# Both batches together, products on two halves of the rows, values and state in blocks of 64 columns

## The chip, the cores and the metric

The kernel runs on one core of a Trainium2 chip. A core has a matrix engine (TensorE, PE in the rows), three engines for elementwise work (VectorE or DVE, ScalarE or ACT, GpSimd or POOL) and SyncE (SP), which here issues all transfers. Each engine works through its own instructions in order and waits on semaphores for others. TensorE multiplies a stationary operand (loaded first, PEld in the rows) with a moving one and adds into banks of its result memory. The metric is the device time of one execution in microseconds (us): 297.85 is the median of 3 runs (297.58 to 298.0).

## The reference

Three steps follow each other, for 2 batches of 768 tokens. The first is a gated memory over time with 8 heads of 40 features:

```
m_new = max(f[t] + m, i[t]);  f_stab = exp(f[t] + m - m_new);  i_stab = exp(i[t] - m_new)
C = f_stab * C + i_stab * outer(v[t], k[t]);   n = f_stab * n + i_stab * k[t]
y[t] = sigmoid(o[t]) * (C @ q[t]) / max(|n . q[t]|, 1)
```

The heads are put side by side as x (320 features). The second step is x + relu(norm(x) @ w_ch1) @ w_ch2, where norm takes mean and variance over the features and w_ch1 is 320 x 1280. The third is h = relu(x @ w_in) with w_in 320 x 1024, a convolution of h over three neighbouring tokens, h * sigmoid(conv), and a product with w_out (1024 x 320). All is float32.

## The kernel before

The 768 tokens are worked through in 6 chunks of 128 (index c) and, within each, in the 2 batches (index b). For a chunk the memory is not stepped token by token: scores of keys against queries (line 491, two heads at a time, one on rows 0 to 39 and one on rows 64 to 103) are multiplied on VectorE by a decay table `wt` (made by line 447 in the first two chunks, by lines 452 and 456 later) and then with the values (line 509, 41 columns a head: 40 and the sum n); the state carried in from earlier chunks adds line 507; line 544 makes the chunk's contribution to the state, and lines 551 and 555 update it. VectorE then normalises (519 to 536), TensorE transposes (570), and ScalarE and VectorE split the result into a high and a low part (574, 575), since the layers multiply in a float32 format with a short fraction: each product is high x high, low x high and high x low.

The first layer (`f1_unit`) works in units u of two blocks f of 128 hidden features, with both batches as 256 moving columns. `first_mm` contracts 320 rows as 128 + 128 + 64; the last 64 share one product with the low parts of the same weights, so a block takes 8 products (lines 583 to 587). ScalarE (607) and VectorE (609) take a unit's bank of 512 columns out, as high and low parts, and `second_mm` (592 to 594) multiplies them with w_ch2, 320 columns a product, 6 products a block, into two banks that collect over all units. Line 636 adds x, line 570 transposes again, and three chunks later (`LAG`) `f2_unit` does the same for the third step, with the convolution on ScalarE, VectorE and GpSimd between (683 to 718). The banks for first products are two, taken in turn (`slots`, "big").

The weights arrive in float64, as pairs of words: lines 343 to 346 turn them into float32, and 369 to 391 split them, during the first half of the time. Transfers are issued by SyncE in order, at line 253.

Every operation is recorded first (`Sched.op`) and then written out in the order of the table `ORDER`, which sets each engine's sequence; a "-" in it is a product with constants (line 802) that keeps TensorE busy at the start. Semaphores are set by the data, whatever the order.

Of the kernel before, what the change touches and what calls it, by code (L numbers as in the profile page):

```python
# [8 lines left out]
F32 = mybir.dt.float32  # L9
# [8 lines left out]
L = 128  # L18
# [6 lines left out]
WARM_START, WARM_END = 950.0, 45000.0  # L25
# [3 lines left out]

ORDER = """
10 6 2 35 11 12 4 14 5 88 44 34 20 95 43 21 160 22 23 102 24 25 - - - - - - - 52 33 26 27 13 19 29 3 28 30 7 159 36
89 116 38 17 37 9 15 45 90 18 281 16 31 39 91 47 8 0 40 46 92 54 55 48 109 53 49 41 93 58 57 32 56 97 276 94 96 69
42 59 294 60 50 51 61 62 63 123 70 98 64 161 65 99 104 71 72 73 66 74 75 100 76 80 103 77 78 67 1 79 - 85 162 68 164
165 82 86 105 173 167 83 87 106 117 84 - - - - 282 163 118 166 245 119 169 107 168 170 81 120 171 181 277 172 283
# [42 lines left out]


class Sched:

    LAT = {"A": dict(A=150, G=175, P=150, S=145, V=180), "V": dict(A=128, G=155, P=130, S=120, V=127),
           "G": dict(A=80, G=80, P=86, S=67, V=80), "P": dict(A=200, G=222, P=2, S=190, V=196),
           "S": dict(A=20, G=20, P=20, S=20, V=20)}

    def __init__(self):
# [783 lines left out]
```

## Time and profile before

| | |
|---|---|
| median of 3 runs | 297.85 us (297.58 to 298.0) |
| profiled execution: span from first to last instruction | 285.8 us |
| around the span (median less span; the page gives the profiled execution no other time of its own) | 12.05 us |
| TensorE busy | 276.1 us (97%), 2180 instructions |
| VectorE, ScalarE, GpSimd busy | 205.4, 176.6, 102.1 us |
| moved by transfers | 34.84 MB |

A product's record reaches from its start to the end of its results, and the next product starts long before that, so the records overlap: what a product costs TensorE is the distance from its start to the next start. In a row of the time line "x16" means that 16 like instructions were merged, and the time is that from the first start to the last end. A granted clock of 1.00 is TensorE's upper level of 2.4 GHz.

### The profile page before, as it was taken

What the parts mean: (1) busy time and instruction counts of PE and PEld (TensorE: products, weight loads), DVE (VectorE), ACT (ScalarE), POOL (GpSimd) and SP (SyncE); (2) the same over time, 40 slices, a digit from 0 to 9 for tenths busy, and PEclk for the clock granted to TensorE, in tenths of its full rate; (3) what the DMA queues carried; (4) which work ended last, traced back from release to release, by engine and by line L of the source; (5) the groups of instructions that cost most, each with busy time, mean ns of one, the idle gap of its engine ahead of it and who ended that gap; (6) DMA issues with size and microseconds to landing.
All of it is one profiled execution on the core that took longest, in us unless ns stands there. A gap on an engine that the chain in (4) does not pass through costs nothing.

```text
span 285.8 us, 5747 instructions
## 1 busy us (share of the span) xinstructions
PE 276.1 (97%) x2180; PEld 265.5 (93%) x2181; DVE 205.4 (72%) x442; ACT 176.6 (62%) x409; POOL 102.1 (36%) x147
## 2 busy tenths in 40 slices
PE   7989999899989999999999999999999999999995
PEld 3977999799989999999999999999999999999994
DVE  5899999974985497668966465785345669797581
ACT  3949877687659449932747635453336358677672
POOL 4514486556556632755020410020100102533540
PEclk9979999999999999999999999999999999999999
DMA  6993977964785487033540000100001000010011
GB/s 267 354 324 102 381 263 275 307 229 167 248 300 145 146 251 238 0 101 102 183 166 27 2 0 2 47 2 0 2 0 46 2 0 3 0 49 0 24 71 46
DMA packets 11860, 34.84 MB, mean 122 GB/s; under 512 B 1431, under 2 KB 5416, under 8 KB 11832
## 3 DMA queue, kind: packets, MB, share of 16 engines
q1 hardware_dynamic: 11832, 34.47, 35.2%
q8 instruction: 17, 0.28, 0.4%
q14 instruction: 11, 0.09, 0.1%
HBM read 32.46 MB, written 2.01 MB: 121 GB/s over the span
## 4 chain that ended last, share of the span: by engine, by line
PE 64%; DVE 23%; ACT 5%; DMA 4%; issue 2%; SPq 0%; POOL 0%; DVEq 0%; POOLq 0%; ACTq 0%
PE bk L592 8%; PE bk L593 8%; PE bk L594 8%; PE bk L583 7%; PE bk L585 6%; PE bk L584 6%; DVE c L555 4%; PE bk L491 4%; PE bk L509 3%; PE bk L586 3%; PE bk L587 3%; DVE xc L536 2%; DVE wt L498 2%; DMA wt<-gd 2%; PE bk L570 2%
## 5 line engine op out<-in xcount | busy, mean ns | idle before, releaser
L592 PE MATMUL bk<-w2h,uh 128*128 128x320 f32 x120 | 38.5, 321 | 0.0
L708 DVE SCALAR_TENSOR_TENSOR scr<-scr,cwr 128x256 f32<-128x256 f32 x70 | 33.5, 518 | 6.0 <-ACT scr L702 5.6
L594 PE MATMUL bk<-w2h,ul 128*128 128x320 f32 x120 | 37.1, 309 | 0.0
L593 PE MATMUL bk<-w2l,uh 128*128 128x320 f32 x120 | 37.0, 309 | 0.0
L583 PE MATMUL bk<-xth,w1h 128*128 128x256 f32 x120 | 35.6, 297 | 0.1
L585 PE MATMUL bk<-xtl,w1h 128*128 128x256 f32 x120 | 33.9, 282 | 0.0
L584 PE MATMUL bk<-xth,w1l 128*128 128x256 f32 x120 | 33.8, 282 | 0.0
L609 DVE SCALAR_TENSOR_TENSOR ul<-bk,uh 128x512 fp32r<-128x512 f32 x30 | 20.5, 687 | 14.4 <-ACT uh L607 14.3
L583 PE MATMUL bk<-rh,wih 128*128 128x256 f32 (+1 forms) x96 | 27.9, 290 | 0.3 <-DVE ul L609 0.3
L346 POOL TENSOR_TENSOR scr<-scr 128x640 int32<-128x640 int32 x14 | 18.4, 1316 | 24.9 <-DVE scr L345 9.7
L585 PE MATMUL bk<-rl,wih 128*128 128x256 f32 (+1 forms) x96 | 27.2, 283 | 0.0
L584 PE MATMUL bk<-rh,wil 128*128 128x256 f32 (+1 forms) x96 | 27.2, 283 | 0.0
L607 ACT ACTIVATE uh<-bk 128x512 fp32r<-128x512 f32 x30 | 17.6, 592 | 15.2 <-PE bk L587 10.3
L684 ACT ACTIVATE scr<-bk 128x512 f32<-128x512 f32 (+2 forms) x29 | 14.9, 518 | 17.3 <-PE bk L587 17.2
L456 ACT ACTIVATE wt<-wt,bcol 128x128 f32<-128x128 f32 x64 | 22.8, 394 | 3.8 <-POOL wt L452 3.7
L509 PE MATMUL bk<-vk,wt 128*128 128x41 f32 x192 | 24.6, 270 | 0.0
L509 PEld LDWEIGHTS bk<-vk,wt 128*128 128x128 f32 x192 | 24.0, 192 | 0.1
L583 PEld LDWEIGHTS bk<-xth,w1h 128*128 128x128 f32 x120 | 22.7, 189 | 0.9 <-DVE ul L609 0.2
L592 PE MATMUL bk<-woh,uh 128*128 128x320 f32 x74 | 23.1, 312 | 0.0
L592 PEld LDWEIGHTS bk<-w2h,uh 128*128 128x128 f32 x120 | 22.5, 188 | 0.5
L593 PE MATMUL bk<-wol,uh 128*128 128x320 f32 x74 | 22.9, 309 | 0.0
L594 PE MATMUL bk<-woh,ul 128*128 128x320 f32 x74 | 22.8, 308 | 0.0
(192 smaller groups left out, 839.6 us busy)
## 6 DMA issues: line engine op xcount, KB each, us to landing
vk<-in_vko_dram SPq DMA_DIRECT2D x12, 528.0 KB, 6.4
xy<-in_kq_dram SPq DMA_DIRECT2D x12, 512.0 KB, 5.0
wt<-gd SPq DMA_DIRECT2D x8, 512.0 KB, 3.7
scr<-in_w_dram SPq DMA_DIRECT2D x6, 640.0 KB, 7.0
stg<-in_w_dram SPq DMA_DIRECT2D x4, 640.0 KB, 12.0
scr<-in_win_dram SPq DMA_DIRECT2D x4, 640.0 KB, 4.2
scr<-in_wout_dram SPq DMA_DIRECT2D x4, 640.0 KB, 4.9
out_dram<-scr SPq DMA_DIRECT2D x12, 160.0 KB, 1.8
```

The lines of the kernel that those rows point to most:

```text
L346: op(G, 80 + 1.78 * n, [(rk, 0)], [(rk, 1)], lambda: gq.tensor_tensor(out=hi, in0=hi, in1=lo, op=ALU.add))
L456: lambda h=h: ac.activation(out=w[:, h, :], in_=w[:, h, :], func=AF.Exp, bias=bcol[:, c * 16 + r0 + h:c * 16 + r0 + h + 1]))
L509: pe.matmul(out=num[:, h * 41:(h + 1) * 41], lhsT=w[:, GROW[h], :], rhs=v1[:, h * 41:(h + 1) * 41], start=(c == 0), stop=(c == 0 or h == m ...
L583: pe.matmul(out=pv, lhsT=wh[:, k, fs], rhs=hi(k), start=(k == 0), stop=False)
L584: pe.matmul(out=pv, lhsT=wl[:, k, fs], rhs=hi(k), start=False, stop=False)
L585: pe.matmul(out=pv, lhsT=wh[:, k, fs], rhs=lo(k), start=False, stop=False)
L592: pe.matmul(out=a, lhsT=hi(b), rhs=wh[:, k, :], start=first, stop=False)
L593: pe.matmul(out=a, lhsT=hi(b), rhs=wl[:, k, :], start=False, stop=False)
L594: pe.matmul(out=a, lhsT=lo(b), rhs=wh[:, k, :], start=False, stop=last)
L607: op(A, da(512, True), [pk], [hk], lambda: ac.activation(out=uh[i], in_=pb, func=AF.Relu))
L609: lambda: ve.scalar_tensor_tensor(out=ul[i], in0=pb, scalar=0.0, in1=uh[i].bitcast(F32), op0=ALU.max, op1=ALU.subtract))
L708: ve.scalar_tensor_tensor(out=cvt()[:, j], in0=h[:, j, :, k:k + 128], scalar=cw_t[:, k, f0 + j:f0 + j + 1], in1=cvt()[:, j], op0=ALU.mult, ...
```

## The change

Each chunk's attention is written once for both batches: `wt`, `qt`, the state, x and their operations hold both, so that elementwise instructions have twice the columns and are half as many, and values, keys and queries come in one transfer for both batches (keys and queries one for each batch, on 40 rows). The 8 banks are 4 pairs (`pp`), one bank of a pair for each batch or block.

The products of the layers, the decay tables, the spread of the running maximum and the transposes are cut into halves of 64 rows, rows 0 to 63 and rows 64 to 127. In `first_mm` and `second_mm` neighbouring instructions belong to different halves and to different banks of a pair; in phase 0 bank 0 takes the lower rows and bank 1 the upper, in phase 1 it is exchanged. 320 rows are 5 blocks of 64: three in one phase, two in the other. `mul` watches each bank: when a product comes from the other half of the rows than the one before it in that bank, an empty instruction of SyncE (`sp.nop`) waits for the last products of both banks, and the new product waits for it. From the second chunk on `f1_unit` takes two units at a time (`QUAD`) into one pair of banks, which it uses alone (`pair("big", [0])`). Values and state (`fnum`, `fst`) keep all 128 rows, and are cut into blocks of 64 result rows (`CB`), that is 64 columns of the stationary operand. The weights of the input layers lie by 64 rows, and one instruction splits them where there were three. The last output is taken out by ScalarE for one batch and by VectorE for the other. `ORDER` is new, with 1008 operations for 1252, and 26 of its entries are products with constants, each now two halves.

```diff
+QUAD = True
+CB = 64
...
+3 5 2 6 19 11 20 21 22 7 13 154 81 23 8 10 24 12 25 155 26 67 28 4 33 27 18 82 68 34 29 138 - - - - - - - - - - 37 36
...
+    pp = [ps.tile([128, 2, 512], F32, name=f"pp{i}", tag=f"pp{i}") for i in range(4)]
...
+    def pair(cls, slots):
+        n = count.get(cls, 0)
+        count[cls] = n + 1
+        i = slots[n % len(slots)]
+        return ("pp", i), pp[i]
...
+    def rows(h):
+        return slice(64 * h, 64 * h + 64)
...
+    def mul(**kw):
+        o, rg = kw["out"], kw["lhsT"].start_partition()
+        k = o.tensor.name, o.offset % 1024 // 512
+        if k in last and last[k][0] != rg and last[k][2] is None:
+            mark = sp.nop()
+            for q in range(2):
+                if (k[0], q) in last:
+                    r, old, _ = last[k[0], q]
+                    after(mark, old)
+                    last[k[0], q] = r, old, mark
+        mark = last[k][2] if k in last and last[k][0] != rg else None
+        ins = pe.matmul(**kw)
+        if mark:
+            after(ins, mark)
+        last[k] = rg, ins, None
...
+        def fnum():
+            for b in range(2):
+                for n in range(3 if c else 0):
+                    for z in range(0, 128, CB):
+                        pe.matmul(out=num[z:z + CB, b, n * 123:(n + 1) * 123], lhsT=qt[:, b, n, z:z + CB], rhs=ct[:, b, n * 123:(n + 1) * 123],
+                                  start=(n == 0), stop=False)
+                for n in range(NH):
+                    for z in range(0, 128, CB):
+                        pe.matmul(out=num[z:z + CB, b, n * 41:(n + 1) * 41], lhsT=w[:, b, GROW[n], z:z + CB], rhs=v1[:, b, n * 41:(n + 1) * 41],
+                                  start=(n == 0 and c == 0), stop=(n == NH - 1))
+        op(P, [(wk, 0), (wk, 1), (vkey, "v")] + (["ct", "qt"] if c else []), [nk], fnum)
...
+            def fst():
+                for b in range(2):
                     for g in range(3):
-                        pe.matmul(out=gb[0:120, g * L:(g + 1) * L], rhs=g80[0:32], start=True, stop=True,
-                                  lhsT=hsel[:, 360 * b + 120 * g:360 * b + 120 * g + 120])
-                op(P, 3 * 224 + 390, ["g80", "hsel"], [gk], feg, act=0.5)
-                op(A, da(384, True), [gk], [(ek, j) for j in range(3)],
...
+    def first_mm(t, pvs, wh, wl, n, hi, lo, ph, first, final):
+        if first:
+            fresh(t)
+        count = [0, 0]
+        for j in range(3 - ph):
+            for x, y in ((wh, hi), (wl, hi), (wh, lo)):
+                for bk in range(2):
+                    r, k = rows(bk ^ ph), ((0, 1, 2), (0, 2, 1))[bk ^ ph][j]
+                    a = x[r, n, j * 256 + bk * 128:j * 256 + bk * 128 + 128] if j < 2 else x[r, n, 512:640]
+                    count[bk] += 1
...
+    def second_mm(acc, hi, lo, wh, wl, fs, ph, first, final):
+        if first:
+            fresh(acc)
+        for n, f in enumerate(fs):
+            for x, y, m in ((hi, wh, 0), (hi, wl, 1), (lo, wh, 2)):
+                for b in range(2):
+                    r = rows(b ^ ph)
+                    mul(out=acc[:, b, 0:DM], lhsT=x(f, b, r), rhs=y[r, f, :],
+                        start=(first and n == 0 and m == 0), stop=(final and n == len(fs) - 1 and m == 2))
+
+    turn = {}
+
+    def phases(which, us):
+        p = turn.get(which, 0)
+        turn[which] = 1 - p
+        return [(u, p) for u in us] + [(u, 1 - p) for u in reversed(us)]
+
+    def f1_unit(c, us):
...
+        pk, pt = pair("big", [0])
+        nq = len(us)
...
+        todo = phases("f", list(range(nq)))
+        for n, (q, ph) in enumerate(todo):
+            u = us[q]
+            op(P, [("xth", c % 2), ("xtl", c % 2), ("w1", "h", u), ("w1", "l", u)], [pk],
+               lambda q=q, u=u, ph=ph, n=n: first_mm(pt, [pt[:, bk, q * 256:(q + 1) * 256] for bk in range(2)], w1h, w1l, u,
...
+    def f2_out(c):
+        a = pp[acc2(c)]
+        dst = out[:, c * L:(c + 1) * L, :].rearrange("b t d -> t b d")
+        if c < NC - 1:
+            op(A, [("pp", acc2(c))], ["ob"], lambda: ac.activation(out=ob, in_=a[:, :, 0:DM], func=AF.Copy, scale=0.5))
+            op(SP, ["ob"], [("out", c)], lambda: sp.dma_start(out=dst, in_=ob))
+        else:
+            op(A, [("pp", acc2(c))], [("ob", 0), "ob"], lambda: ac.activation(out=ob[:, 0], in_=a[:, 0, 0:DM], func=AF.Copy, scale=0.5))
+            op(V, [("pp", acc2(c))], [("ob", 1), "ob"] if 0 else [("ob", 1)],
+               lambda: ve.tensor_scalar(out=ob[:, 1], in0=a[:, 1, 0:DM], scalar1=0.5, scalar2=None, op0=ALU.mult))
             for b in range(2):
-                for j in range(nf):
```

In TensorE's order a second layer's products and a first layer's, in the fourth chunk of the first layer. Before (`bk_136` and `bk_137` collect the second products of the two batches, `bk_132` is one of two banks for first products):

```order
L592 MATMUL bk_136<-w2h,uh_125 128x320 [waits Activation_49]
L593 MATMUL bk_136<-w2l,uh_125 128x320
L594 MATMUL bk_136<-w2h,ul_129 128x320 [waits DVE_49]
L592 MATMUL bk_137<-w2h,uh_125 128x320
L593 MATMUL bk_137<-w2l,uh_125 128x320
L594 MATMUL bk_137<-w2h,ul_129 128x320
L583 MATMUL bk_132<-xth_117,w1h 128x256
L584 MATMUL bk_132<-xth_117,w1l 128x256
L585 MATMUL bk_132<-xtl_119,w1h 128x256
```

After, near the same place (`pp_111` is the pair for first products, `pp_113` and `pp_114` collect second products; line 233 is `mul`):

```order
L233 MATMUL pp_111<-xth_104,w1h 128x256 x2
L233 MATMUL pp_111<-xth_104,w1l 128x256 x2
L233 MATMUL pp_111<-xtl_106,w1h 128x256 x2
L233 MATMUL pp_114<-woh,uh 128x320 [waits SP_sequencer_49]
L233 MATMUL pp_114<-woh,uh 128x320
L233 MATMUL pp_114<-wol,uh 128x320 x2
L233 MATMUL pp_114<-woh,ul 128x320 x2
L233 MATMUL pp_114<-woh,uh 128x320 x2
L233 MATMUL pp_114<-wol,uh 128x320 x2
L233 MATMUL pp_114<-woh,ul 128x320 x2
L233 MATMUL pp_111<-xth_104,w1h 128x256 [waits SP_sequencer_49]
L233 MATMUL pp_111<-xth_104,w1h 128x256
```

Products now stand in twos, one of each half of the rows; a phase of second products (12 instructions) stands between the two phases of a first layer's unit, and both it and the second phase wait for SyncE.

The values of one chunk, before, for the first of the two batches (`c_96` is its state, `qt_88` its queries) up to where the other batch's begin:

```order
L507 MATMUL bk_135<-c_96,qt_88 128x123 [waits DVE_49,Pool_49]
L509 MATMUL bk_135<-vk_87,wt_92 128x41 [waits DMAHW4_49]
L509 MATMUL bk_135<-vk_87,wt_92 128x41 x2
L507 MATMUL bk_135<-c_96,qt_88 128x123
L509 MATMUL bk_135<-vk_87,wt_92 128x41 x3
L507 MATMUL bk_135<-c_96,qt_88 128x123
L509 MATMUL bk_135<-vk_87,wt_92 128x41 x2
L507 MATMUL bk_134<-c_97,qt_89 128x123 [waits DVE_49]
```

After, for both batches (line 472 is the state's part, line 476 the scores'):

```order
L472 MATMUL pp_112<-ct,qt 64x123 [waits DVE_49,Pool_49]
L472 MATMUL pp_112<-ct,qt 64x123 x5
L476 MATMUL pp_112<-vk_85,wt 64x41 [waits DMAHW1_49]
L476 MATMUL pp_112<-vk_85,wt 64x41 x15
L472 MATMUL pp_112<-ct,qt 64x123 x6
L476 MATMUL pp_112<-vk_85,wt 64x41 x16
```

Each product of 128 result rows has become two of 64, and the two batches follow each other in one group.

SyncE's issues in the first part of the program, before:

```order
L253 DMA scr<-in_w_dram 128x1280 [waits DMAHW7_49,DVE_49,Pool_49]
L336 DMA gd<-g_80 80x128 [waits DMAHW0_49,DVE_49]
L253 DMA scr<-in_w_dram 128x1280 [waits DMAHW1_49,DVE_49,Activation_49]
L253 DMA vk_85<-in_vko_dram 128x1056 [waits DMAHW2_49,PE_49]
L253 DMA xy_82<-in_kq_dram 128x1024 [waits DMAHW3_49]
```

After:

```order
L243 DMA scr<-in_w_dram 128x1280 [waits PE_49,DMAHW2_49,DVE_49,Activation_49]
L243 DMA stg_71<-in_w_dram 128x1280 [waits DMAHW3_49,DVE_49]
L314 DMA gd<-g_80 64x128 [waits PE_49,DMAHW4_49]
L243 DMA stg_72<-in_w_dram 128x1280 [waits DMAHW5_49,DVE_49,Activation_49]
L243 DMA vk_84<-in_vko_dram 128x2112 [waits DMAHW6_49,PE_49]
L243 DMA kq<-in_kq_dram 40x2048 [waits PE_49,DMAHW7_49]
```

There are 66 issues and the like instead of 88 rows, and a wait for PE in front of an issue is often that of an exchange signal, which the rows don't show by itself, standing in the queue between two issues.

## Rows read from the trace of the kernel before

**Rows 1.** The page: busy us and share of TensorE, and the chain's shares by engine.

```profile
PE 276.1 (97%) x2180; PEld 265.5 (93%) x2181; DVE 205.4 (72%) x442; ACT 176.6 (62%) x409; POOL 102.1 (36%) x147
PE 64%; DVE 23%; ACT 5%; DMA 4%; issue 2%; SPq 0%; POOL 0%; DVEq 0%; POOLq 0%; ACTq 0%
```

**Rows 2.** Stages: length; busy PE, PEld, DVE, ACT, POOL; granted clock; DMA share; GB/s.

```profile
0.00:23.40 23.40, 20.63 (x144) 15.81 (x145) 18.62 (x57) 14.39 (x29) 9.77 (x19) 0.93 0.89 311
23.40:60.00 36.60, 35.05 (x285) 32.26 (x285) 33.93 (x60) 29.98 (x67) 22.09 (x20) 1.00 0.76 270
60.00:160.00 100.00, 98.01 (x806) 95.87 (x805) 73.28 (x169) 63.67 (x165) 44.14 (x60) 1.00 0.47 155
160.00:282.50 122.50, 122.46 (x952) 121.60 (x951) 79.60 (x161) 68.12 (x150) 26.14 (x49) 1.00 0.04 15
```

**Rows 3.** Time line of TensorE at 161 us: start, us, engine, line, operation.

```profile
160.96 0.28 PE L587 MATMUL bk<-xtl,w1h 128*128 128x256 f32 x1
161.08 0.31 PE L592 MATMUL bk<-woh,uh 128*128 128x320 f32 x1
161.22 0.31 PE L593 MATMUL bk<-wol,uh 128*128 128x320 f32 x1
...
161.81 0.31 PE L594 MATMUL bk<-woh,ul 128*128 128x320 f32 x1
162.05 1.16 PE L491 MATMUL bk<-xy 40*128 40x128 f32 x16
163.14 0.39 PE L583 MATMUL bk<-rh,wih 128*128 128x256 f32 x1
163.36 0.28 PE L584 MATMUL bk<-rh,wil 128*128 128x256 f32 x1
```

**Rows 4.** The page's groups: busy us, mean ns, idle before and its releaser.

```profile
L592 PE MATMUL bk<-w2h,uh 128*128 128x320 f32 x120 | 38.5, 321 | 0.0
L583 PE MATMUL bk<-xth,w1h 128*128 128x256 f32 x120 | 35.6, 297 | 0.1
L609 DVE SCALAR_TENSOR_TENSOR ul<-bk,uh 128x512 fp32r<-128x512 f32 x30 | 20.5, 687 | 14.4 <-ACT uh L607 14.3
L607 ACT ACTIVATE uh<-bk 128x512 fp32r<-128x512 f32 x30 | 17.6, 592 | 15.2 <-PE bk L587 10.3
```

**Rows 5.** Time line of TensorE: values and state, at 12 and at 177 us.

```profile
12.61 0.88 PE L544 MATMUL bk<-vk 128*120 128x123 f32 x6
13.32 1.88 PE L509 MATMUL bk<-vk,wt 128*128 128x41 f32 x16
...
177.21 0.38 PE L507 MATMUL bk<-c,qt 120*128 120x123 f32 x2
177.42 0.76 PE L509 MATMUL bk<-vk,wt 128*128 128x41 f32 x6
...
179.58 0.37 PE L583 MATMUL bk<-xth,w1h 128*128 128x256 f32 x1
```

**Rows 6.** Time line at 148 us, where TensorE waits for VectorE.

```profile
148.57 0.69 DVE L609 SCALAR_TENSOR_TENSOR ul<-bk,uh 128x512 fp32r<-128x512 f32 x1 [1.60 <-ACT uh L607]
149.31 0.19 PEld L583 LDWEIGHTS bk<-rh,wih 128*128 128x128 f32 x1 [0.55 <-DVE ul L609]
149.31 0.39 PE L583 MATMUL bk<-rh,wih 128*128 128x260 f32 x1 [0.34 <-DVE ul L609]
```

**Rows 7.** Time line of the end.

```profile
282.11 0.83 ACT L740 ACTIVATE scr<-bk 128x320 f32<-128x320 f32 x2 [2.60 <-PE bk L594]
282.15 0.31 PE L594 MATMUL bk<-woh,ux 128*128 128x320 f32 x1
282.57 0.81 SPq L742 DMA_DIRECT2D out_dram<-scr  x2
```

**Rows 8.** The first layer's start in the time line.

```profile
23.36 0.39 PE L583 MATMUL bk<-xth,w1h 128*128 128x256 f32 x1
```

**Rows 9.** The page's transfers: count, KB each, us from issue to landing.

```profile
vk<-in_vko_dram SPq DMA_DIRECT2D x12, 528.0 KB, 6.4
...
stg<-in_w_dram SPq DMA_DIRECT2D x4, 640.0 KB, 12.0
```

More of the change, by code (lines that the diff above doesn't have):

```diff
@@ L109, in op @@
         deps.discard(i)
-        self.ops.append((eng, dur, deps, fn, dma))
-        if port is None:
-            port = not dma and dur > 0 and (eng == "G" or eng == "V" and not any(
-                isinstance(k, tuple) and k[0] == "bank" for k in list(reads) + list(writes)))
-        self.port.append(port)
-        if eng == "P":
-            self.act[i] = act
-    def chain(self, eng, steps, reads, writes, port=None):
-        for dur, fn in steps:
-            self.op(eng, dur, reads, writes, fn, port=port)
+        self.ops.append((eng, deps, fn))
     def emit(self, warm):
@@ new lines, in sm, with after @@
+    def sm(c):
+        return pair("sm", [1, 3]) if c <= 3 else pair("sm1", [1])
+    def rows(h):
+        return slice(64 * h, 64 * h + 64)
+    last = {}
+    def after(ins, old):
+        tc.add_manual_dep(ins.ins, old.ins.name, mybir.DependencyInfo(mybir.DependencyClass.Sync, mybir.DependencyReason.DATA))
+    def mul(**kw):
[13 more added lines that the diff above has]
+        last[k] = rg, ins, None
@@ L259, in consts, with fresh, load @@
+    def fresh(t):
+        for q in range(2):
+            last.pop((t.tensor.name if hasattr(t, "tensor") else t.name, q), None)
+    def load(dst, src, key, reads=(), e=None):
+        op(SP, list(reads), [key] if not isinstance(key, list) else key, lambda: (e or sp).dma_start(out=dst, in_=src))
+    op(V, [], ["one"], lambda: ve.memset(one, 0.0))
+    op(A, [], ["one"], lambda: ac.activation(out=one, in_=one, func=AF.Exp))
+    load(early[1][0:16, 0:2 * S], gf, "fi")
     def consts():
         make_identity(nc, ident)
-    op(G, 510, [], ["ident"], consts)
@@ L340, in convert, with spread @@
-    def convert(raw, n, rk):
+        load(f80, gf80, "f80")
+        mk, mb = sm(0)
+        m80 = mb[0:80, 0, 0:256].rearrange("p (k t) -> p k t", k=2)
+        def spread():
+            fresh(mb)
+            for k in range(2):
+                for n, c in enumerate(LATER):
+                    mul(out=m80[:, k, :], lhsT=zsel[:, 64 - 16 * n:144 - 16 * n], rhs=mm[:, c * L + k:(c + 1) * L + k],
+                              start=(n == 0), stop=(n == NC - 2))
+        op(P, ["m0", "m1", "mm0", "zsel"], [mk], spread)
@@ new lines, in gates_rest, with feg @@
+        gk, gb = sm(0)
+        def feg():
+            fresh(gb)
+            for g in range(3):
+                for b in range(2):
+                    mul(out=gb[0:120, b, g * L:(g + 1) * L], rhs=g80[64:128], start=True, stop=True,
+                              lhsT=hsel[:, 360 * b + 120 * g:360 * b + 120 * g + 120])
+        op(P, ["g80", "hsel"], [gk], feg)
+        op(A, [gk], EG,
+           lambda: ac.activation(out=eg, in_=gb[0:120, :, 0:384].rearrange("p b (g t) -> p b g t", g=3), func=AF.Exp))
@@ L606, in f1_unit @@
[L606 to L616 removed]
+        un[0] += nq
@@ L667, in f2_unit @@
         if c % 2:
-            rd = [r for r in rd if r[1] == 1] + [("r", 0, "x", 0), ("r", 0, "x", 1)]
-        pk, pb = pbank("big" if c < NC - 3 else "end")
-        late = c >= NC - 3
+            rd = [r for r in rd if r[1] == 1] + [("r", 0, "x")]
+        late = c >= NC - LAG
+        pk, pt = pair("end", [0, 1]) if late else pair("big", [0])
         i = un[0] % (9 if late else 4)
@@ L752, in dst_x @@
-    def dst_x(c, b):
-        sl = slice(b * 128, (b + 1) * 128)
-        return (lambda: xth[c % 2][:, :, sl], lambda: xtl[c % 2][:, :, sl], ("xth", c % 2, b), ("xtl", c % 2, b))
-    xinfo = {}
-    def attn(c):
-        todo = [attention(c, b, dst_x(c, b)) for b in range(2)]
-        while todo:
-            todo = [t for t in todo if next(t, 0) is None]
-    attn(0)
+    load(gln_t, gln.partition_broadcast(128), "gln")
+    attention(0)
     weights1()
     gates_rest()
-    load(cwr.rearrange("p n k -> p (n k)"), cw.bitcast(I32), [("cwr", 0), ("cwr", 1)], 128 * 192)
@@ L767, in tile_kernel, with zero_tail @@
-    convert(cwr, 24, "cwr")
-    op(G, 0, [("cwr", 1)], ["cw"], lambda: None)
+    load(cwr.rearrange("p n k -> p (n k)"), cw.bitcast(I32), [("cwr", 0), ("cwr", 1)])
+    convert(cwr, "cwr")
+    op(G, [("cwr", 1)], ["cw"], lambda: None)
     weights2()
+    def zero_tail():
+        gq.memset(rh()[:, :, :, 257:258].bitcast(F32), 0.0)
+        gq.memset(rl()[:, :, :, 257:258].bitcast(F32), 0.0)
     for s in range(NC + LAG):
-        a = [("a", u) for u in range(5)] if s < NC else []
-        f = f2_units(s - LAG) if s >= LAG else []
+        a = ([(n,) for n in range(5)] if s == 0 or not QUAD else [(0, 1), (2, 3), (4,)]) if s < NC else []
+        f = range(4) if s >= LAG else []
@@ L800, in tile_kernel @@
     with tc.manual_schedule():
         def warm():
-            pe.matmul(out=bank[7], lhsT=wz[:, 0:128], rhs=wz, start=True, stop=True)
-        sch.emit((WARM_START, WARM_END, warm))
+            for i in range(2):
+                mul(out=pp[2][:, i], lhsT=wz[rows(i), 0:128], rhs=wz[rows(i)], start=True, stop=True)
+        sch.emit(warm)
 _OUTS = [((2, 768, 320), 'float32')]
```

777 lines of the change are left out of this document (339 added, 438 removed), and 73 rows, old and new, of the table ORDER.

## The prediction, made before the result was known

> **What bounds the kernel now.** I read the page's busy shares first, then the chain that ended last, then a table of stages, then the time line of TensorE in the dense part. TensorE is busy for 276.1 of 285.8 us, and it holds 64% of the chain; VectorE, the next, holds 23% [rows 1]. A busy TensorE is not yet a TensorE at its limit, so the stages decide. Up to 23.40 us it waits for the head (transfers, the gate scan, the first chunk) and for its clock (granted 0.93); from 23.40 to 60.00 us VectorE works 33.93 of 36.60 us beside it; from 60.00 us on TensorE works 98.01 of 100.00 and then 122.46 of 122.50 us, at a granted clock of 1.00 (2.4 GHz), and VectorE has a third of its time free [rows 2]. So from 60 us on the sum of TensorE's steps is the time, and before that nearly so. The step from one start to the next is what counts, not the record's length, since records overlap: a first product (256 columns) takes 0.12 us, a second product (320 columns) 0.146 us (5 steps from 161.08 to 161.81) [rows 3]. The difference, 0.027 us for 64 columns, is 0.42 ns a column, so a first product is 0.107 us of columns and 0.013 us of something between two products.
>
> The page gives the profiled execution's span, 285.8 us; the median of the runs is 297.85, so 12.05 us lie around the span. I add the terms to the span and keep those 12.05 us.
>
> **The change, part by part.** All steps are between starts, in us.
>
> *First products.* Before, 8 in each of 108 blocks (60 of the first layer, as x120 with two a block shows, and 48 of the second) [rows 4]: 864 x 0.120 = 103.7. The 64 left-over rows share one product with their own low parts. After, the 5 blocks of 64 rows give 15 products for each bank, two at a time on the two halves of the rows: 54 units x 15 = 810 pairs. What a pair costs no row shows in this type. The nearest rows: the score products already run in pairs on rows 0 to 39 and 64 to 103, and 16 of them take 1.16 with their last record of 0.27, 0.89 for 8 pairs, 0.111 a pair [rows 3]; a whole product of the type in question costs 0.120. They are equally near (one has the tiling, the other the type), so I take the middle, 0.1155: 93.6, **-10.1**, with ends -13.8 and -6.5.
>
> *Second products.* 108 blocks x 6 = 648 steps before and 648 pairs after, so only the 0.013 between products is at stake: with the score pairs' 0.004 a step is 0.137, else 0.147; middle 0.142, **-3.3**, ends -6.5 and 0.
>
> *Values and state in halves of 64 columns.* Before, the values of one batch and chunk take 2.37 (177.21 to 179.58), 10 times, and 16 x 0.11 without the state term, 2 times; the state takes 0.88 less its last record, 0.7, 10 times [rows 5]: 34.2. A 41-column step costs 0.11 although its columns last 0.034 (twice 41 at 0.42 ns; two passes in this type), so the load of 128 columns sets it. A half loads 64 columns, 0.058. If the halves run beside each other as the score pairs do, a batch and chunk has 16 x 0.058 + 6 x 0.109 = 1.58, the first chunk 0.93, the state 0.65: 15.8 + 1.9 + 6.5 = 24.2, **-10.0**. If their loads go one after the other: 22 x 0.111 = 2.44, and 34.7 in all, +0.5. If nothing overlaps: 3.17, 3.7 and 13.1, +14.3. I take the first, by the score pairs' row, the only one in which TensorE is divided.
>
> *Changes of the tiling.* From the last whole product at 161.81 to the second at 163.36 one visit to the score pairs lasts 1.55; its steps are 0.147 + 8 x 0.111 + 0.120 = 1.155 [rows 3]. So two changes cost 0.40. In the order such changes fall from 30 to 18 (scores, transposes and layers now share one tiling): **-2.4**.
>
> *The exchange waits (new).* Each bank takes its first half of a sum from one half of the rows and the rest from the other. Between them TensorE signals SyncE, which signals back: 93 times. I counted in the order what TensorE does between, at the steps above: nothing in 13 cases, at least 0.66 us in 80. The price with nothing between: the last record 0.31, a hop 0.05 each way (VectorE's result ends at 149.26, the load starts at 149.31), SyncE's own step (no row shows one; between nothing and the 0.40 of an issue [rows 7], near nothing, 0.03, as it moves no data), the bare load 0.11 (the first record after a wait is 0.39, not 0.28), less the step of 0.147 [rows 3, 6]: 0.40. So 13 x 0.40 = **+5.2**; the 0.66 covers the price of the others. Ends +2.6 (half of it lies in waits that are there anyway) and +15 (0.12 for each covered one as well, the bare load alone).
>
> *One pair of banks for the first products (new).* Before, two banks take turns; after, a unit of 1024 columns fills both, and the next must wait for ScalarE and VectorE. By twice the 512-column rows that is 1.18 + 1.37 [rows 4], with record, hops and bare load under 3.0. The order puts 0.8 to 5.0 us of second products and attention between; over the 36 hand-overs some 3 us stay open: **+3.0**, ends 0 and +8. Both engines have room from 60 us on [rows 2].
>
> *The end and the head.* Before, the first batch's output leaves while the second is computed, ScalarE ends 0.5 us after the last product and two issues take 0.81 [rows 7]. After, both batches end together and the issues follow: **+0.4**. The first layer starts at 23.36 us [rows 8] behind the transfer of values and the chain on VectorE; after, the merged transfer (twice 528 KB [rows 9]) stands behind an exchange wait on SyncE, while the key transfers shrink. I take **0**, with 2 either way.
>
> *VectorE and ScalarE* do the same columns in fewer instructions. It costs nothing while TensorE covers them, and shortens the 23 to 60 us stage, where VectorE would else be next.
>
> Sum: -10.1 - 3.3 - 10.0 - 2.4 + 5.2 + 3.0 + 0.4 = -17.2. Span 268.6, time **280.6 us**.
>
> **The rivals.**
> 1. *Pairs without the gap.* If the pairs of the layers step like the score pairs, the two product terms are -20.3 instead of -13.4: 273.7 us. For it: the tiling is the same. Against: the gap of 0.013 belongs to the layers' type.
> 2. *The halves of 64 columns don't run beside each other.* Their outputs share a bank and their inputs the same rows, which no row before shows. With loads in turn the term is +0.5: 291.1 us; with nothing overlapping 304.9. Against: the loads of whole value products already hide behind products on the same rows, since a step of 0.11 is the load alone, not 0.107 + 0.034 [rows 5].
>  The Trainium skill ("TensorE: Matmul & The Clock Gate", Part 3, on what overlaps) says that a load overlaps running products only where the row group differs; by it the halves, which share all rows, would wait for each other and this rival would hold. The trace of before disagrees for whole products, and no row shows it for halves.
> 3. *Slower: the exchange waits stand in SyncE's queue behind transfers.* That queue goes in order, and 30 of the 93 signals follow an issue that itself waits for a buffer or an earlier transfer. If TensorE reaches the second half first, it stands for the rest of that wait; a landing takes 6.4 us for the values and 12.0 us for staged weights [rows 9]. It decides from 17.2 us: three or four such stops of 4 to 5 us. With 20 us the time is 300.6. For it: transfers are busy for half of the first 160 us (0.89, 0.76, 0.47) [rows 2]. Against: most issues wait for things that are long done when TensorE gets there, and from 160 us on the share is 0.04.
> 4. *The change doesn't do what it says:* two halves in the layers' type never run at once. Then 1458 pairs become 2916 steps, about +180 (1458 more at some 0.12): 460 us. The score pairs speak against it.
>
> **How the numbers follow.** Forecast 0.45 (own range 274 to 288, from the ends of the product and exchange terms); rival 1 0.26; rival 2 0.14; rival 3 0.13; rival 4 0.02. The forecast and rival 1 are faster; of rival 2 0.08 is still faster by over 0.2%, about what a measurement of this kernel can tell from no change, and 0.02 within it; I leave 0.01 of the forecast within it too. Faster 0.78, same 0.03, slower 0.19. For 8 in 10 the range goes from 267 (rival 1 with cheaper exchanges) to 299 (most of rival 2, the beginning of rival 3).
>
> **What would show it right or wrong.** In the profile after: pair steps of the layers between 0.111 and 0.120 and between 0.137 and 0.147; value steps of 41 columns at 0.06 a pair of halves, not 0.11; gaps of about 0.4 us on TensorE in front of 13 second halves and none in front of most others; a TensorE whose idle time is spread in small pieces. The forecast fails if a value pair takes 0.11 or more, if SyncE holds TensorE for microseconds, or if the dense part is set by VectorE or ScalarE.

## The result, and the profile after

The kernel after takes 287.68 us (median of 4, 286.36 to 289.03), the kernel before 297.93 in the same comparison (297.58 to 298.45): a ratio of 0.9657, 95% interval 0.9614 to 0.9699. Forecast were 280.6 and a range of 267 to 299. The sign and the range held, but much of the working behind them did not. One thing must be known to read the number: executions of the kernel before fall in two groups, 286 to 292 us and 295 to 301 (28 and 55 of the 83 that the experiments timed); all four in the comparison are of the long group, and the profile shown before the prediction is of the short one.

The kernel after, its page: busy time of the engines with share of the span, and the chain that ended last by engine, to be read against [rows 1].
```profile
span 287.3 us, 9346 instructions
...
PE 268.4 (93%) x4057; PEld 252.1 (88%) x4057; DVE 197.8 (69%) x343; ACT 164.3 (57%) x316; POOL 102.6 (36%) x133
...
PE 60%; DMA 13%; ACT 11%; DVE 8%; issue 4%; POOL 3%; SPq 1%; POOLq 0%; ACTq 0%; DVEq 0%
```
TensorE is 7.7 us less busy than before and yet the span is 1.5 us longer than the 285.8 of [rows 1]. Transfers hold 13% of the chain that ended last, where they held 4%. The stages say where the time went. The kernel after, by stretch; PEclk is the granted clock as a share of 2.4 GHz, the figures behind it the transfers' share and GB/s.
```profile
0.00:23.20 23.20, 15.88 (x170) 10.96 (x172) 13.04 (x29) 11.67 (x17) 9.31 (x19) 0.89 0.86 282
23.20:36.80 13.60, 12.98 (x126) 11.52 (x124) 8.67 (x25) 6.76 (x12) 3.74 (x3) 0.68 0.64 170
36.80:60.00 23.20, 23.00 (x379) 21.51 (x377) 17.15 (x26) 16.50 (x25) 14.35 (x11) 1.00 0.80 270
60.00:160.00 100.00, 96.26 (x1600) 92.92 (x1598) 76.25 (x118) 58.96 (x124) 50.26 (x56) 1.00 0.45 148
160.00:283.00 123.00, 120.31 (x1800) 115.23 (x1798) 82.21 (x147) 69.97 (x139) 24.90 (x45) 1.00 0.06 20
```
The first layer starts at 36.78 us, not at 23.36 [rows 8]. Up to 23.2 TensorE works 15.9 us, and from there to 36.8 at a clock of 0.68. This is the way there; TensorE, ScalarE (ACT), GpSimd (POOL) and SyncE's issues in the head of the kernel after, in order of engine.
```profile
14.95 0.85 PE L507 MATMUL pp<-vk 128*64 128x123 f32 x12 [0.36 <-POOL vk L449]
20.16 1.49 PE L507 MATMUL pp<-vk 128*64 128x123 f32 x12 [4.36 <-POOL half L261]
21.44 3.59 PE L476 MATMUL pp<-vk,early 128*64 128x41 f32 x64
...
36.78 0.28 PE L233 MATMUL pp<-xth,w1h 64*128 64x256 f32 x2
...
16.86 0.76 ACT L335 ACTIVATE stg<-stg 128x640 f32<-128x640 f32 x1 [4.70 <-DMA stg<-in_w_dram]
...
18.20 0.75 ACT L452 ACTIVATE vk<-vk 128x640 f32<-128x640 f32 x1
...
13.86 1.03 POOL L449 TENSOR_TENSOR vk<-vk,d 128x360 f32<-128x360 f32 x1 [2.07 <-DMA vk<-in_vko_dram]
...
19.02 1.09 POOL L449 TENSOR_TENSOR vk<-vk,d 128x360 f32<-128x360 f32 x1 [3.98 <-ACT vk L452]
...
7.54 0.36 SPq L243 DMA_DIRECT2D vk<-in_vko_dram  x1
```
Read from the bottom: the values of chunk 0 are issued at 7.54, behind two weight blocks and an exchange mark (before: 2.58), and GpSimd, which waits for them, starts at 13.86. ScalarE waits 4.70 us for a weight block; the tanh on the output gate, queued behind it, starts at 18.20. GpSimd's second scaling of the keys waits for that tanh, although it touches other columns. By the code, both batches now share one tile, and the gate's stretch over both encloses the second batch's keys; e3 moves that tanh. TensorE stands from 15.8 to 20.16 for it. Behind this wait the clock stands at its lower level (0.51 on average from 18 to 32), and the 64 value products take 3.59 us; in e3_gate_early, below, at the higher level they take 2.01.

The dense part of the kernel after: first products, second products, carried state (123 columns) and values (41).
```profile
48.48 0.86 PE L472 MATMUL pp<-ct,qt 120*64 120x123 f32 x12
49.17 1.08 PE L476 MATMUL pp<-vk,wt 128*64 128x41 f32 x32
50.07 0.83 PE L472 MATMUL pp<-ct,qt 120*64 120x123 f32 x12
...
53.20 0.28 PE L233 MATMUL pp<-xth,w1l 64*128 64x256 f32 x2
53.32 0.29 PE L233 MATMUL pp<-xtl,w1h 64*128 64x256 f32 x2
53.45 0.30 PE L233 MATMUL pp<-w2h,uh 64*128 64x320 f32 x2
53.59 0.31 PE L233 MATMUL pp<-w2l,uh 64*128 64x320 f32 x2
53.74 0.31 PE L233 MATMUL pp<-w2h,ul 64*128 64x320 f32 x2
```
A pair of first products steps by 0.12, a pair of second ones by 0.146, hardly less than the whole products of [rows 3]. A batch's 16 value products, as 32 halves, go by in 0.90 (49.17 to 50.07): 0.056 a pair of halves, against 0.11 [rows 5]. The forecast of the halves was right, and the Trainium skill ("TensorE: Matmul & The Clock Gate", Part 3, on what overlaps), by which a load overlaps running products only where the row group differs, does not hold here: all these halves use the same rows, and 0.056 is half of what an undivided product takes.

The kernel after, what the weight loads waited for (us in all, times, longest).
```profile
PEld pp L233 <- SPq L226: 4.7, 14, 0.4
PEld pp L507 <- POOL half L261: 4.6, 1, 4.6
...
PEld pp L233 <- DVE ul L598: 2.9, 6, 0.8
```
14 exchanges cost 4.7 us, 0.34 each, none over 0.4. The 6 waits for VectorE's low part (`ul`) are first products that wait for the one pair of banks; this hand-over costs 2.9. Those were the steps of +5.2 and +3.0.

### The profile page after: what moved, and what is told of

Read it like the earlier page. It is cut to its first block, busy times and chain, and to the rows that moved or that the text cites. A ratio compares the mean times of both kernels' runs of the same rounds, so it can differ in the third digit from the quotient of the medians.

```text
span 287.3 us, 9346 instructions
## 1 busy us (share of the span) xinstructions
PE 268.4 (93%) x4057; PEld 252.1 (88%) x4057; DVE 197.8 (69%) x343; ACT 164.3 (57%) x316; POOL 102.6 (36%) x133
## 4 chain that ended last, share of the span: by engine, by line
PE 60%; DMA 13%; ACT 11%; DVE 8%; issue 4%; POOL 3%; SPq 1%; POOLq 0%; ACTq 0%; DVEq 0%
PE pp L233 53%; DMA scr<-in_win_dram 7%; ACT wt L434 3%; PE pp L476 3%; DMA early<-in_kq_dram 3%; DVE ul L598 2%; ACT uh L596 2%; DMA scr<-in_w_dram 2%; PE pp L472 2%; PE pp L507 1%; POOL qt L443 1%; DMA qt<-in_q3t_dram 1%; SPq L243 1%; DVE cvx L691 1%; DVE wt L465 1%
## 5 line engine op out<-in xcount | busy, mean ns | idle before, releaser
L233 PE MATMUL pp<-xth,w1h 64*128 64x256 f32 x300 | 44.7, 289 | 0.5 <-DVE ul L598 0.3
L691 DVE SCALAR_TENSOR_TENSOR scr<-scr,cwr 128x256 f32<-128x256 f32 x72 | 33.2, 507 | 16.2 <-ACT scr L686 15.9
L233 PE MATMUL pp<-xtl,w1h 64*128 64x256 f32 x300 | 43.1, 278 | 0.0
L233 PE MATMUL pp<-xth,w1l 64*128 64x256 f32 x300 | 43.1, 278 | 0.0
L233 PE MATMUL pp<-w2h,uh 64*128 64x320 f32 x240 | 38.8, 314 | 0.2 <-SPq L226 0.2
L233 PE MATMUL pp<-rh,wih 64*128 64x256 f32 (+1 forms) x240 | 37.0, 295 | 2.0 <-DVE ul L598 1.0
L233 PE MATMUL pp<-w2l,uh 64*128 64x320 f32 x240 | 37.9, 306 | 0.0
L233 PE MATMUL pp<-w2h,ul 64*128 64x320 f32 x240 | 37.9, 306 | 0.0
L233 PE MATMUL pp<-rl,wih 64*128 64x256 f32 (+1 forms) x240 | 35.4, 280 | 0.4 <-DVE rl L545 0.4
L233 PE MATMUL pp<-rh,wil 64*128 64x256 f32 (+1 forms) x240 | 35.1, 278 | 0.0
L233 PEld LDWEIGHTS pp<-xth,w1h 64*128 64x128 f32 x300 | 29.1, 185 | 2.3 <-DVE ul L598 0.7
```

The lines of the kernel that those rows point to most:

```text
L233: ins = pe.matmul(**kw)
L691: lambda k=k, j=j: ve.scalar_tensor_tensor(out=cvt()[:, j], in0=h[:, j, :, k:k + 128], scalar=cw_t[:, k, f0 + j:f0 + j + 1], in1=cvt()[:, ...
```

## The experiments

**e1, e5: the kernel before again.**

> The kernel before, unchanged, to see the span and the granted clock of its timed executions, which the profile shown (span 285.8 us) doesn't tell. If the 12.05 us that I kept around the span are real, the timed executions have spans of 285 to 287 us at a clock of 0.99. If the profiled execution was simply shorter than the timed ones, the spans are 294 to 296 us, with 2 to 3 us around them as in the kernel after; then the right base of the prediction is about 295, not 285.8, and what the change takes away inside the span is about 10 us. The profile of this run then shows where the timed executions lose 10 us against the first profile.

> The kernel before again (a comment line added), one look. Its executions fall in two groups, near 287.5 and near 297 us (e1_before: 286.3 to 288.6 and 296.1 to 298.3); both profiles so far are of the lower group. Theory: in the upper group TensorE's clock stands at its lower level for some 20 us in the middle, behind the value and state products of one chunk, as in the one profile of e2_undivided (0.50 from 108 to 121 us); a profile of 296 to 298 us then shows such a stretch, and all other stages as before. Rival: the clock is as in the first profile, and the 10 us are lost to transfers or other waits, at full clock.

> The same as e5_look_a, another look: the same two theories. A profile of the lower group (286 to 289 us) tells neither.

e1: 10 executions, 6 at 286.3 to 288.5 and 4 at 297.6 to 298.3; the profile is a short one (287.83, span 286.0), so 1.8 us lie around the span, not 12.05. Of the two single executions one came out short (e5_look_a, 287.22, span 285.4), one long (e5_look_b, 298.18, span 296.4). TensorE in the short one:
```profile
4.94 1.16 PE L491 MATMUL bk<-xy 40*128 40x128 f32 x16 [1.02 <-DMA xy<-in_kq_dram]
...
10.80 1.98 PE L509 MATMUL bk<-vk,wt 128*128 128x41 f32 x16
...
23.20 0.38 PE L583 MATMUL bk<-xth,w1h 128*128 128x256 f32 x1
```
and in the long one:
```profile
0.77 3.15 PE L802 MATMUL bk<-const-bfloat16-1.0 128*128 128x512 bf16 x7 [0.77 <-PEq L861]
5.16 2.08 PE L491 MATMUL bk<-xy 40*128 40x128 f32 x16 [1.24 <-DMA xy<-in_kq_dram]
...
16.20 3.63 PE L509 MATMUL bk<-vk,wt 128*128 128x41 f32 x16
...
34.17 0.39 PE L583 MATMUL bk<-xth,w1h 128*128 128x256 f32 x1
34.39 0.28 PE L584 MATMUL bk<-xth,w1l 128*128 128x256 f32 x1
```
The same products take nearly twice as long in the long execution up to about 33 us, and the usual 0.28 from 34 on: after the 7 fillers (products with constants) and the gap of 1.24 us the clock never rose to its higher level in the head. (The page's clock row reads 9 there, since the record of the clock has no event before 32.8; the steps show it.) The first layer starts 10.97 us later; from there to the last product both executions take the same 258.9. So the theory was half right: it is the clock, but in the head, not in the middle. The rival, a full clock and other waits, is what the clock row alone would have suggested, and is out.

**e8: is it the gap behind the start fillers?**
```diff
-24 25 - - - - - - - 52 33
+24 25 - - - - - - - - - - 52 33
```


> The kernel before with 10 instead of 7 filler products at its start, nothing else changed: 7 end at 3.92 us and leave TensorE idle until the keys land (4.87 to 5.16); in the long execution of e5_look_b the clock stands at its lower level until 32.8, in the short ones it rises at 4.3 to 4.6. Theory: the two groups of the kernel before come from this gap, so with it closed the clock rises in every execution and all times are 286 to 289 us, none at 296 to 298. Rival: it is the narrow value products behind it (41 columns, and steps of 0.11) or the moment of the start that decide, and the upper group stays, in about two of three executions.

287.71 us (median of 12), ratio to short executions of before 0.9968 (0.9916 to 1.002): ten at 286.9 to 289.0, to which the ratio belongs, and two at 295.1 and 296.1, while the unchanged kernel beside it was long in 16 of 24. In the profile the fillers now reach up to the first score product, and the gap is closed. The mean granted clock of the single executions tells two sorts of long ones apart, which the theory did not foresee. Of the 16, 14 have 0.998 to 1.0, as e5_look_b (0.999) has, since its record lacks the slow head; 2 have 0.96. With three more fillers none of the first sort is left among 12, and both long ones are of the second (0.959 and 0.965). Of all 55 long executions 11 are of this second sort; none was profiled, so where their clock was low stays open. The run does not separate the gap from the longer start: the fillers close the one and lengthen the other, and e6, below, has a gap of 1.15 us and no long execution among 12.

**e10: the kernel after again, beside it.**

> The kernel after again (a comment line added), timed in the same call as e8_before_filler and e9_head. Theory: against executions of before at the same clock the change brings nothing measurable: its dense part is 12.7 us shorter (246.2 instead of 258.9 from the first layer's first product to the last product), its head 13.6 longer; so it comes out at 286 to 289, within 1 us of e8_before_filler, and the gain of 10.3 us lies in the clock of the head of before. Rival: it is 3 us or more faster than e8_before_filler.

290.14 us (median of 12, 284.6 to 295.0): 1.1 above 289.0, the median of the eight short executions of before beside it, and 2.4 above e8. The ratio to short executions of before, 0.9914 (0.9816 to 1.0012), holds for its three shortest executions alone. No gain can be told. The rival of 3 us is out, and the theory's 286 to 289 is missed by 1.1. Its profile (291.68) is one of the longer ones, and shows one reason why it scatters (columns as above):
```profile
64.00:66.00 2.00, 0.79 (x12) 0.53 (x8) 0.03 (x1) 2.00 (x8) 1.89 (x2) 1.00 0.65 178
66.00:68.00 2.00, 0.00 (x0) 0.00 (x0) 1.06 (x3) 2.00 (x6) 1.58 (x2) 0.52 0.10 28
68.00:73.00 5.00, 4.98 (x46) 4.99 (x48) 3.69 (x5) 4.97 (x14) 2.07 (x3) 0.51 0.00 2
```
TensorE waits 3.2 us, up to 68.0, for a split of operands on VectorE (L545); the clock falls at 66 and 5 us of products at half speed follow the wait.

**e2, e6: the column halves, taken away and alone.** e2 sets `CB = 128` in the kernel after; e6 puts into the kernel before, in the three loops of lines 507, 509 and 544, the like of
```diff
-pe.matmul(out=num[:, h * 41:(h + 1) * 41], lhsT=w[:, GROW[h], :], ...
+for z in (0, 64):
+    pe.matmul(out=num[z:z + 64, h * 41:(h + 1) * 41], lhsT=w[:, GROW[h], z:z + 64], ...
```


> The kernel after with the value and state products of all chunks on 128 columns again, not in two halves of 64; all else as it is. Theory: halves run beside each other, so a product of 41 columns for both halves takes 0.058 us and an undivided one 0.111; the time rises by 8 to 11 us over the kernel after, to 296 to 299. Rival: where these products stand TensorE waits for something else, so the time rises by less than 3 us. Second rival: the halves bring nothing (steps of 0.11 for a pair): no change, within 1 us.

> The kernel before with one part of the change alone: value and state products in two halves of 64 columns beside each other, all else (order, whole-row products of the layers) as before. Theory: the part is worth 8 to 10 us against executions of before at the same clock, 277 to 280 us instead of 287.5, and where the value stretches are what the clock falls behind, the upper group near 297 goes as well. Rival: each stretch has work for other engines behind it (the score multiplication, the normalisation), and the time saved turns into waits: 285 us or more in the lower group, and the upper group stays.

e2: 300.27 us (median of 4, 294.7 to 307.5), 12.6 above the kernel after (10.1 above its 290.14 in e10); this is near the theory's 8 to 11, its 296 to 299 is missed by 1.3, and both rivals are out. The step is back at 0.112; for the 160 steps from the first layer on that is 160 x 0.054 = 8.6 us. In the profiled execution, the longest of the four (307.54), the clock fell once more, at 107.9, behind a wait of 2.10 us for GpSimd's scaled queries, through a stretch of carried state and values; what takes the rest in the other three no profile shows.
```profile
105.00:110.00 5.00, 2.90 (x22) 2.69 (x20) 1.75 (x2) 1.82 (x2) 4.18 (x3) 0.79 0.04 11
110.00:115.00 5.00, 5.00 (x25) 5.00 (x25) 0.93 (x1) 1.40 (x2) 0.19 (x1) 0.50 0.69 262
```
e6: 288.46 us (median of 12, 285.2 to 289.0), ratio to short executions of before 0.9985 (0.9911 to 1.006). The second batch's value products of chunk 0, from 17.4 on at the higher clock, and the first layer's start:
```profile
17.23 1.16 PE L511 MATMUL bk<-vk,wt 128*64 128x41 f32 x32
...
25.98 0.39 PE L586 MATMUL bk<-xth,w1h 128*128 128x256 f32 x1
```
Value steps are 0.058, but from the first layer on the products take 257.3 instead of 258.9. Without waits the values and the carried state save 7.2 us. Of this 2.9 come back as waits (7.2 us beyond 0.25 in TensorE's steps instead of 4.3), 1.5 in the state's products, which take longer in halves (6.3 instead of 4.8), and 1.3 in the layers' steps. So the rival was right on the time of the short group, and its reason, waits, is the largest of three. On the long group the theory was right: none of 12 is there, though 13 of 17 of the unchanged kernel beside it were. The part that the forecast priced at -10.0 gives next to nothing in the kernel before, and yet removes its long executions; how it does so its profile only suggests: there too the clock was low (7.2 to 17.4 us), but it rose again at the value products of chunk 0, and the first layer started at 25.98.

**e7: second products whole.** One product on 128 rows for each pair:
```diff
-for n, f in enumerate(fs):
...
-r = rows(b ^ ph)
-mul(out=acc[:, b, 0:DM], lhsT=x(f, b, r), rhs=y[r, f, :], ...)
+f = fs[ph]
...
+mul(out=acc[:, b, 0:DM], lhsT=x(f, b, slice(0, 128)), rhs=y[:, f, :], ...)
```


> The kernel after with the second products on all 128 rows again (648 whole products in place of 648 pairs, the same order, one half of a unit's products in each of its two places); so 39 of the 93 exchanges go, and every place where first and second products meet changes the tiling. By the steps of the traces a whole product takes 0.146 and a pair 0.1447, so the products themselves cost +0.8; the exchanges in front of second halves that nothing covers give back about 2 to 3. Theory: a change of tiling costs 0.20 here too; with some 100 more of them the time rises by 15 to 20 us. Rival: a change costs nothing beside the bare load where products follow each other at once, and the time is within 2 us of the kernel after.

306.4 us (median of 4, 305.1 to 308.1), ratio to short executions of before 1.0623 (1.0522 to 1.0724), 18.7 us above the kernel after (16.3 above its 290.14 in e10): the theory's 15 to 20. The step of a whole product is 0.147, of a pair 0.146. TensorE where first products end and whole second ones begin, two to a row, and the waits of the loads:
```profile
200.69 0.29 PE L233 MATMUL pp<-xtl,w1h 64*128 64x256 f32 x2
200.91 0.56 PE L233 MATMUL pp<-w2h,uh 128*128 128x320 f32 x2
201.31 0.46 PE L233 MATMUL pp<-w2l,uh 128*128 128x320 f32 x2
201.61 0.46 PE L233 MATMUL pp<-w2h,ul 128*128 128x320 f32 x2
```
```profile
PEld pp L233 <- issue: 11.0, 58, 0.2
```
The step at the change is 0.22 instead of 0.12, and the next two take 0.40 instead of 0.30: 0.2 us a change, as estimated. From the first layer on the products take 267.7 instead of 246.2; at most 3.4 of these 21.4 can be the clock, which was low once from 34.2 to 41.0. The Trainium skill ("TensorEngine Tiling (Array Packing)", Key Properties) says that changing the tiling mode drains TensorE; these rows agree and give the price. So dividing the second products gains nothing in itself; it saves the changes that divided first products would else bring.

**e3, e4, e9, e11: the head.** All are the kernel after with its order table edited. e3 moves the tanh (45) ahead of the weight conversion that waits (89); e4 puts 16 fillers ahead of the state products (62); e9 issues keys and values first and puts the conversions behind the attention of chunk 0; e11 is e9 with 14 fillers behind the spread (140) and one half unit (250) ahead of a transposition.
```diff
 e3
-74 31 85 89 95 267 46 - - - - - - 86 45 43
+74 31 45 85 89 95 267 46 - - - - - - 86 43
 e9, the start
-3 5 2 6 19 11 20 21 22 7 13 154 81 ... 67 28 4 33 27 18 82 68 34 29 138
+3 5 2 33 34 35 6 19 11 20 21 22 7 13 154 81 ... 67 28 4 27 18 29 138
```


> One ScalarE instruction moved: the tanh on the output gate of chunk 0 stands ahead of the conversion of a weight block instead of two instructions behind it. In the kernel after the conversion waits 4.7 us for its transfer, the tanh behind it starts at 18.20, GpSimd's second scaling of the keys waits for the tanh (19.02), TensorE's state products for that (20.16), and the clock is at its lower level from 18.1 to 31.8. Theory: this queue is what delays TensorE; with the tanh ahead the second scaling ends near 16, the state products go on at 16, the idle time of 4.4 us is under 1, and the time falls by 4 to 9 us (the wait, and the part of the stretch at the lower clock that goes with it). Rival: the gates of the other chunks or the weights' transfers are next, and the first layer starts at 36 us as before: under 1 us.

> The kernel after with 16 more filler products (32 half products on constants, some 4 us at the full clock) on TensorE ahead of the state products of chunk 0, where it waits 4.4 us; no wait is removed. Theory: only the lower clock is at stake: it stays at its higher level, the work from 20.2 to 31.8 us takes about half of its 11.6, and the time falls by 4 to 6 us. Rival: that stretch waits for other engines and transfers, and TensorE at the higher level only waits more: within 1 us, or up to 1 us slower for the filler.

> The kernel after with another order of its first 81 operations alone: the transfers of keys and values of chunk 0 go out ahead of the first two weight blocks and of any exchange mark on SyncE; on ScalarE, VectorE and GpSimd the conversions of weight blocks stand behind the attention of chunk 0 (the gate's tanh, the scaling of the keys, the score multiplication, the state's mask). TensorE's order is unchanged. Theory: the head of the kernel after is a queue problem, and the first layer starts at 27 to 29 us instead of 36.8 (e3: 33.1): 278 to 281 us. Rival: the first layer's weights, now issued later, are what it waits for, or the time is given back between 40 and 100 us, where transfers run at 60 to 90 per cent: 284 to 288 us.

> The kernel of e9_head with 14 more filler products (28 half products, some 3.5 us at the full clock) behind the spread of the gate states, where TensorE waits from 21.5 to 25.0 us for VectorE's gate scan, and with one half of a second product's unit moved ahead of the transposition of chunk 1, where it waits 1.3 us. No wait is removed. Theory: in e9_head the clock falls to its lower level from 26.0 to 32.9 behind that wait, and 6.8 us at half speed cost 3.4; kept up, the first layer starts at 29 us and the time falls by 3 to 4 us from the profile of e9_head (span 280.9), to spans of 277 to 278 and times of 279 to 280; and the scatter of e9_head (282.7 to 290.6), if it comes from falls of the clock behind waits, gets smaller. Rival: the clock falls elsewhere instead, or what is won in the head is waited for at the weights between 40 and 100 us: 282 to 285 as e9_head.

Against short executions of before, with the number of their own executions that the ratio takes in: e3 287.03 us, ratio 0.9908 (0.9851 to 0.9966), 10 of 10; e4 285.37, 0.9856 (0.9754 to 0.9958), 4 of 4; e9 285.32, 0.9849 (0.9749 to 0.995), 4 of 6; e11 284.6, 0.9813 (0.9644 to 0.9981), 4 of 6 (and two of before).

In e3 the state products go on at 16.21, and the first layer starts 3.7 us earlier:
```profile
16.21 0.86 PE L507 MATMUL pp<-vk 128*64 128x123 f32 x12 [0.34 <-POOL half L261]
16.91 2.01 PE L476 MATMUL pp<-vk,early 128*64 128x41 f32 x64
...
33.07 0.28 PE L233 MATMUL pp<-xth,w1h 64*128 64x256 f32 x2
```
From there to the last product it takes 246.1 us, as the kernel after does (246.2), so nothing of this is waited for again; the end takes 0.9 more, and the profiled spans are 284.3 and 287.3. The medians differ by 0.65 only (287.03 and 287.68), less than the theory's 4 to 9: the profiled execution of the kernel after is the longest of its four (289.03). In e4, e9 and e11 too the products take 245.5, 245.2 and 246.5 from the first layer on. What the head wins is kept in all four profiles.

e4 starts the first layer at 33.9; its four executions (283.8 to 286.0) all lie below the shortest of before beside them (287.8). It is 2.3 below the 287.68 of the kernel after, less than the theory's 4 to 6. In its profile the clock already stood at its lower level from 7.2 to 17.4 us, ahead of the new fillers, so that the gain can't be put down to them alone. e9, the head as ordered anew:
```profile
19.07 2.43 PE L233 MATMUL pp<-const-bfloat16-1.0 64*128 64x512 bf16 x19
24.97 1.30 PE L233 MATMUL pp<-g,early 64*120 64x128 f32 x9 [3.46 <-DVE g L285]
...
31.47 0.42 PE L233 MATMUL pp<-xth,w1h 64*128 64x256 f32 x2
```
The first layer starts at 31.5 instead of 27 to 29: a wait of 3.46 for VectorE's gate scan took the place of the old one, and the clock was low from 26.0 to 32.9. The theory's 278 to 281 fell. The time is in the rival's 284 to 288, but not by the rival's way, since the dense part gives nothing back. e11 fills that wait, and
```profile
25.03 1.24 PE L233 MATMUL pp<-g,early 64*120 64x128 f32 x9 [0.45 <-DVE g L285]
...
28.18 0.61 PE L233 MATMUL pp<-ctmp,identb 64*128 64x512 bf16 x2 [1.22 <-ACT eg L330]
...
31.84 0.42 PE L233 MATMUL pp<-xth,w1h 64*128 64x256 f32 x2
```
the clock falls 2 us later, at 28.0, in another wait (1.22), and the first layer starts no earlier. Its theory of 279 to 280 fell, and the scatter (281.5 to 289.2) is no smaller; the rival, another fall of the clock and 282 to 285, was right. e9 stands 4.8 below the median of the kernel after beside it (285.32 and 290.14), but with 282.7 to 290.6 and 284.6 to 295.0 they overlap.

## Why the prediction was right in sign and wrong in its steps

That the sign and the range held was luck in good part: all four executions of before in the comparison were long ones, and against short ones the change brings nothing measurable (e10). I compare the short execution of before (e5_look_a) with the profile after by the steps from one start to the next over all products of TensorE.

- *"I add the terms to the span and keep those 12.05 us"*: **wrong, and the largest error.** Around the span lie 1.8 us (e1). The other 10 were the clock in the head of long executions (e5_look_b), which the profile, a short one, could not show; the distance between a profile's span and the median of the runs should have been a question, not a constant.
- *The head at 0 ±2*: **wrong.** 36.8 instead of 23.2, +13.6 against a short execution, +2.6 against a long one. The doubt named (values behind an exchange mark) is in the rows, but what held TensorE for 4.4 us was ScalarE's queue; and the wait costs twice, since the clock falls in it, at 18.1, and stays low to 31.8.
- *The dense part*: from the first layer's first product to the last, 246.2 instead of 258.9, **-12.7**; the terms of the forecast that lie in this stretch sum to some -15.8. Of the 12.7, 3.3 are decay and gate products that now come ahead of the first layer.
 - First products: 864 steps of 0.120 became 810 of 0.118, -8.1 (forecast -10.1). Second: 648 of 0.147 became 648 of 0.146, -0.6 (forecast -3.3). The pairs hardly lose the gap between products: the row of the same type told more than the row of the same tiling, and rival 1 is out. So is rival 4, since a pair takes 0.118 and not twice 0.12.
 - Values and carried state 24.0 to 16.6, -7.4 (forecast -7.9 for this stretch), the state 4.8 to 5.7, +0.9 (forecast -0.4): -6.5 (forecast -10.0 in all, of which some 1.8 lie in the head). The mechanism was right and rival 2 is out; the 123-column pairs gain little, 0.105 against 0.112, and those of the state nothing.
 - Tiling changes -2.4: scores and transposes take 3.7 less, in which the divided transposes are not told apart from the changes; 0.2 a change holds (e7).
 - Exchanges and the bank, +5.2 and +3.0: measured 4.7 and 2.9 by the waits. With the bare loads behind them, what first and second products take beyond the steps above grew by 9.4.
 - These make -8.1 - 0.6 + 9.4 - 6.5 - 3.7 - 3.3 = -12.8.
- *Rival 3* (SyncE's queue) did not come on TensorE's exchanges, none over 0.4 us; its like came in ScalarE's queue.

In sum: -12.7 in the dense part, +13.6 in the head and +0.9 at the end (forecast +0.4; from the last product to the end of the span 4.2 instead of 3.3) are +1.8 against a short execution (spans 285.4 and 287.3, rounded); with +2.6 for the head they are -9.2 against a long one (296.4 and 287.3), and the medians differ by 10.3. So the measured gain is there because none of the four executions of the kernel after was of the long group's 295 to 301; of the twelve in e10 one reaches it (295.0). Why is settled in part: three more start fillers take most of the long group away without the change (e8), the column halves all of it (e6); the kernel after has both, more filler at the start (to 4.9 us instead of 3.9) and halves. Which of the two does it there, no run separates.

## What to carry to other kernels

Where the profiled span and the median of the runs differ by several us, time the kernel again and find the profile of the slower execution before any forecast: here, by e10, the whole measured gain lay in that distance. Price a wait in a thinly filled head with the clock that falls behind it, and look through the queue of every engine for an instruction that stands behind a wait for a transfer. Dividing products into halves shortens the step where the load sets it (41 columns) and not where the columns do (256, 320); what that is worth depends on the waits behind it (12.6 us in e2, nothing that can be told in e6).

## What was not expected of the hardware

- Two halves of 64 columns on the same rows run beside each other: 0.058 us a pair, 0.111 undivided.
- An exchange through SyncE with no other work between costs TensorE 0.34 us (4.7 in 14).
- After a start of 7 fillers and 1.0 to 1.2 us of nothing the clock rose in some executions of the same program and not in others; where it did not, it stayed low until 33 us by the products' steps, though TensorE was busy for nearly all of it (10.00 of 10 us from 10 to 20).
